# Head-mixing attention and a gated feed-forward on one core: another order for the first loads, another place for the decoding of w_out, another draw of the planner

## The chip, the cores and the metric

One core of a Trainium2 chip runs one program. The metric is the device time of one execution in microseconds (us). Lower is better.

## The reference

Twelve attention heads are mixed with each other by two small 12 x 12 matrices, once ahead of the softmax and once behind it. The result goes through a two-layer feed-forward whose weights are 64-bit floating-point numbers.

```
q, k, v: 4 batches x 12 heads x 448 tokens x 64        w_pre, w_post: 12 x 12
scores = scale * q @ k^T                   (per head)
scores = einsum('bhij,hg->bgij', scores, w_pre)
attn   = softmax(scores, axis=-1)
attn   = einsum('bhij,hg->bgij', attn, w_post)
x      = (attn @ v), heads put side by side            1792 tokens x 768
h      = x @ w_in                                       768 x 2048
g      = h * clip(h + 3, 0, 6) / 6
out    = g @ w_out                                      2048 x 768
```

## The kernel before

**Work and tiles.** The attention runs in 32 units of about 60 tokens (8 per batch). For a unit `m` and each of 3 pairs of head pairs `p`, `scores` multiplies queries by keys on TensorE (L448), copies the result to an SBUF tile `s` (L470 and L471 for the first two units, on ACT and DVE; L473 on ACT for the rest) and sends it by DMA (L480) into `T_two` or `T_one`, where the heads of one token stand in neighbouring partitions. Twelve such sends of 105 KB make up a unit. Even units use `T_two`, odd ones `T_one`. `step` then takes tokens in tens: the mix ahead of the softmax on TensorE (L533), the maximum of each row on DVE (L541, `nb`), the exponential on ACT (L542), the scaling on POOL (L551), from step 24 on a split into two fp16 numbers (L553 ACT, L554 POOL), the mix behind it on TensorE (L570), and the copy into `AR` (L579 DVE, L581 ACT). `av` multiplies by v (L607). `moe1` is the first feed-forward product (L828), its results go to device memory (`gd`). The second product is L1109: seven products of halves in place of eight, for which sums and differences of blocks of w_out are stored (`wsd`) and read back.

**Weights.** The 64-bit weights are decoded on the core. `w_in_item` loads one of 16 pieces of 786 KB (L354) into a buffer `stw` of which there are two; `decode` takes one ACT pass (L676) and four DVE passes (L679, L683, L687, L691). `w_out_decode` does the same for 24 pieces of 524 KB, with further DVE sums (L781) and stores (L778). Both weights and the first loads of `g` share the two `stw` buffers.

**What sets the order.** Nothing is written in the order in which it runs. Every operation is handed to `Plan` with an engine, a planned duration and a priority (a lower number goes first; most are the step's number plus an offset). `Plan.schedule` walks through planned time and gives each engine, whenever it is free, the ready operation with the lowest number. The result is a fixed order for each engine, the DMA queue of SP among them, in which every transfer waits behind the one ahead of it. Two settings bend the order: `DRAWS`, the seed of a random addition of up to 0.3 to every priority, and `STAY`, by how much TensorE may prefer an operation of the kind that it has just done.

**Fillers.** Where the planner sees TensorE idle between planned us 9 and 150, `filler` puts in matmuls of 512 columns on an identity matrix (L873) that compute nothing. Their number is fixed when the program is built.

**The start.** `mixes` loads the two small matrices and the identity; `keys(0)` and `queries(0, 0)` load the first batch's keys in four transfers and the first queries in two, of which the first holds unit 0 and the second unit 1. Ahead of all that TensorE runs ten matmuls on zeros (L856). `mixes_post` brings the maximum of w_post across partitions with one matmul (`across`, L379, `wst`).

Of the kernel before, what the change touches and what calls it, by code (L numbers as in the profile page):

```python
# [14 lines left out]
F32 = mybir.dt.float32  # L15
# [3 lines left out]
AF = mybir.ActivationFunctionType  # L19
# [8 lines left out]
P = 128  # L28
# [33 lines left out]
DRAWS, JITTER = (3,), 0.3  # L62
AV_BY = 1
Z_AT = 30
LAT_0, ACT_T = 1.0, 1
# [54 lines left out]
class Plan:  # L120
# [7 lines left out]
    STAY = (8.0,)  # L128
# [176 lines left out]
def body(ctx: ExitStack, tc: tile.TileContext, q4, kT, vj, wpre0, wpost0, ident0, w_in, w_out, outT):  # L305
# [85 lines left out]
    def mixes():  # L391
        dma(32768, lambda: SP.dma_start(wpre8(), wpre0), [], [wpre8], -11)
        dma(30720, lambda: SP.dma_start(wpost_n(), wpost0), [], [wpost_n], -10.9)
        dma(32768, lambda: SP.dma_start(ident(), ident0), [], [ident], -10.8)
        dve(0.2, lambda: DVE.tensor_scalar(wpre8(), wpre8(), 1.0 / 8.0, None, op0=ALU.mult), [], [wpre8], -6)
# [16 lines left out]
    def keys(b):  # L412
        for j in range(2):
            t = buf(one, [P, 3, S], F32, f"ks{j}", f"ks_{b}_{j}")
            ks[b, j] = t
            for lo, hi in ((0, 2), (2, 3)) if j == 0 else ((0, 1), (1, 3)):
                (bulk if b or j else dmas)(229376 * (hi - lo), lambda lo=lo, hi=hi, t=t: t()[:, lo:hi], kT[b, :, 3 * j + lo:3 * j + hi],
                                           [(t, i) for i in range(lo, hi)], b * STEPS - 30 + 3 * j + lo if b else -14 + 3 * j + lo)

    def queries(b, c, at, after=()):  # L420
        t = buf(rot, [P, QX], F32, "qx", f"qx_{b}_{c}", 2)
        qs[b, c] = t
        if b + c:
            bulk(P * QX * 4, t, q4[b, c], [t], at, after)
        else:
            for i, (lo, hi) in enumerate(((0, 6 * CU + 4), (6 * CU + 4, QX))):
                dmas(P * (hi - lo) * 4, lambda lo=lo, hi=hi: t()[:, lo:hi], q4[b, c, :, lo:hi], [(t, i)], at + 2.5 * i, after)
# [23 lines left out]

    def scores(m, p, at):
# [16 lines left out]
        if m < 2:  # L469
            act(0.48, lambda: ACT.activation(st()[:, 0], at2[0](), AF.Copy), [ps[0]], [(st, 0)], at + 0.5)  # L470
            dve(0.57, lambda: DVE.tensor_copy(st()[:, 1], at2[1]()), [ps[1]], [(st, 1)], at + 0.5)  # L471
        else:
            act(0.9, lambda: ACT.activation(st(), two()[:, :, :S], AF.Copy), ps, [(st, 0), (st, 1)], at + 0.5)  # L473
        parts = [(0, 10, 6, 0)] if n < 7 else [(0, 10, 2, 0), (20, 5, 2, 2)]
        for cc in range(2):
            for u in range(2):
                h = 2 * (2 * p + cc) + u
                for q0, r, t, t0 in parts:
                    def go(cc=cc, u=u, h=h, q0=q0, r=r, t=t, t0=t0):
                        (ACT if m < ACT_T and u else SP).dma_start(T()[4 + h:4 + h + 12 * (r - 1) + 1:12, t0:t0 + t], st()[D * cc + q0:D * cc + q0 + r * t, u, :])  # L480

                    plan.op("ACT" if m < ACT_T and u else "SP", 0.77, go, [(st, u), T_zero[m % 2]], [(T, (h, t0))], at + 0.7, (), t * 30700, lat=LAT_T if m else LAT_0)
# [394 lines left out]

    plan.filler = filler
    mixes()
    keys(0)  # L880
    queries(0, 0, -13.5)
    for m in range(2):
        for p in range(3):
            scores(m, p, -10 + 8 * m + 1.6 * p)
        if m == 0:
            mixes_post(last_qk)
    for fc in range(EARLY):
        w_in_item(fc)
    FU = [m // 8 * STEPS + 6 * (m % 8) for m in range(NU)]
# [3 lines left out]
    for s in range(NS + 12):  # L893
# [21 lines left out]
        if s in range(WO_AT, WO_AT + WO_BY * WO_EARLY, WO_BY):  # L915
            w_out_decode((s - WO_AT) // WO_BY, 2000 + 10 * (s - WO_AT) // WO_BY, [t_load[s]])
# [312 lines left out]
```

## Time and profile before

| | us |
|---|---|
| median of 3 runs | 797.62 |
| fastest and slowest of them | 796.53, 798.78 |
| the profiled execution | 795.99 |
| its span | 794.2 |
| TensorE busy in it | 774.1 |
| DVE, ACT, POOL busy | 581.2, 527.1, 369.9 |

The span runs from the first to the last instruction of the core; 1.8 us of the profiled execution lie around it. Busy times are those of instructions that compute; issuing a DMA and waiting are not counted. A line such as L533 is a line of the kernel before; in the kernel with the change the same code stands some lines further down (L350 is L351, L480 is L482, L533 is L541, L873 is L881).

### The profile page before, as it was taken

How to read it: one execution, taken by the hardware profiler on the slowest of the kernel's cores; microseconds unless marked ns; L12 is line 12 of the kernel's file. 1: busy time of each engine (PE TensorE's matmuls, PEld its weight loads, DVE VectorE, ACT ScalarE, POOL GpSimd, SP SyncE). 2: the span in 40 equal slices, each digit the busy share in tenths (PEclk: the TensorE clock that was granted, in tenths of full speed). 3: DMA queues.
4: the chain of work that ended last, by engine and by line, in shares of the span. 5: the costliest groups of instructions: out<-in, count | busy, mean ns of one | idle time of the engine just before them, and what ended most of it. 6: DMA issues, size and time to landing. Idle time of an engine off the chain costs nothing.

```text
span 794.2 us, 28021 instructions
## 1 busy us (share of the span) xinstructions
PE 774.1 (97%) x11616; PEld 627.0 (79%) x11616; DVE 581.2 (73%) x1152; ACT 527.1 (66%) x1044; POOL 369.9 (47%) x535
## 2 busy tenths in 40 slices
PE   6999999999999999999999999999999999999998
PEld 2566676678677777777787777768999999999998
DVE  2799796688969368778756678777777599898622
ACT  2588888698998658988775788896676474243200
POOL 2357789479988327767562676886100000000000
PEclk9999999999999999999999999999999999999999
DMA  7766654766365578665746676644599674654101
GB/s 232 211 214 197 204 172 119 215 221 210 90 191 154 155 248 272 209 184 171 231 149 232 193 228 198 197 128 142 178 350 369 215 238 126 186 158 145 42 17 50
DMA packets 100815, 147.75 MB, mean 186 GB/s; under 512 B 9840, under 2 KB 79824, under 8 KB 100688
## 3 DMA queue, kind: packets, MB, share of 16 engines
q1 hardware_dynamic: 100268, 145.31, 58.9%
q8 instruction: 91, 1.49, 0.8%
q10 hardware_dynamic: 420, 0.65, 0.3%
q14 instruction: 36, 0.29, 0.1%
HBM read 76.02 MB, written 31.20 MB: 135 GB/s over the span
## 4 chain that ended last, share of the span: by engine, by line
PE 76%; DMA 7%; DVE 6%; ACT 6%; POOL 2%; issue 2%; SPq 1%; ACTq 0%; POOLq 0%; DVEq 0%
PE single L1109 24%; PE single L828 20%; PE single L570 8%; PE single L607 7%; PE pair L448 7%; PE single L533 6%; PE single L873 3%; DMA T_two<-s 2%; DMA wsd_P<-WF 2%; ACT e L542 2%; DVE nb L541 2%; SPq L480 1%; ACT s L473 1%; ACT eh L553 1%; POOL e L551 1%
## 5 line engine op out<-in xcount | busy, mean ns | idle before, releaser
L828 PEld LDWEIGHTS <-wi 128*128 128x128 f16 x2304 | 213.1, 98 | 24.2 <-issue 18.4
L828 PE MATMUL single<-x,wi 128*128 128x208 f16 (+1 forms) x2304 | 228.5, 259 | 2.0 <-ACT e L542 0.9
L554 POOL TENSOR_TENSOR el<-e,eh 128x448 f16<-128x448 f32 x156 | 168.3, 1097 | 32.0 <-ACT eh L553 30.0
L551 POOL TENSOR_SCALAR e<-e,r 128x448 f32<-128x448 f32 x180 | 129.8, 731 | 39.4 <-DVE r L545 34.4
L1109 PEld LDWEIGHTS <-ws_P 128*128 128x128 f16 x1440 | 138.0, 98 | 0.0
L542 ACT ACTIVATE e<-single,nb 128x448 f32<-128x448 f32 x180 | 113.8, 641 | 20.2 <-DVE nb L541 19.9
L541 DVE TENSOR_REDUCE nb<-single 128x1 f32<-128x448 f32 x180 | 102.9, 614 | 18.5 <-PE single L533 11.0
L553 ACT ACTIVATE eh<-e 128x448 f16<-128x448 f32 x156 | 88.0, 584 | 16.6 <-POOL e L551 16.0
L841 ACT ACTIVATE g<-single,three,uh 128x240 f32<-128x240 f32 (+1 forms) x128 | 68.8, 542 | 41.5 <-PE single L828 41.0
L473 ACT ACTIVATE s<-pair 128x896 f32<-128x896 f32 x90 | 82.9, 921 | 16.4 <-PE pair L448 11.7
L448 PE MATMUL pair<-ks,qx 64*64 64x448 f32 x728 | 89.5, 554 | 3.7 <-ACT s L473 3.6
L843 DVE SCALAR_TENSOR_TENSOR g<-g,six,single 128x240 f32<-128x240 f32 (+1 forms) x128 | 56.2, 442 | 41.3 <-ACT g L841 40.9
L570 PEld LDWEIGHTS <-eh 60*128 60x128 f16 x2496 | 66.3, 100 | 22.3 <-issue 21.4
L607 PEld LDWEIGHTS single<-AR,v 128*64 128x64 f32 (+1 forms) x1536 | 66.8, 136 | 14.3 <-issue 5.2
L607 PE MATMUL single<-AR,v 128*64 128x120 f32 (+3 forms) x1536 | 72.3, 263 | 0.6 <-ACT e L542 0.3
L570 PE MATMUL single<-wpost_h,eh 60*128 60x60 f16 x1248 | 72.4, 202 | 0.3 <-DVE x L633 0.3
L570 PE MATMUL single<-wpost_h,el 60*128 60x60 f16 x1248 | 72.3, 202 | 0.0
L570 PE MATMUL single<-wpost_l,eh 60*128 60x60 f16 x1248 | 72.1, 202 | 0.0
L1109 PE MATMUL single<-gx_P,ws_P 128*128 128x224 f16 x720 | 69.3, 259 | 0.0
L579 DVE TENSOR_SCALAR AR<-single 128x480 f32<-128x480 f32 (+1 forms) x92 | 57.9, 639 | 11.9 <-PE single L570 11.8
L581 ACT ACTIVATE AR<-single 128x480 f32<-128x480 f32 (+1 forms) x92 | 53.5, 586 | 18.7 <-PE single L570 18.7
L544 POOL TENSOR_SCALAR sm<-sm 128x2 f32<-128x2 f32 (+1 forms) x92 | 26.6, 289 | 82.3 <-ACT e L542 77.1
(240 smaller groups left out, 1161.1 us busy)
## 6 DMA issues: line engine op xcount, KB each, us to landing
T_two<-s SPq DMA_DIRECT2D x186, 105.0 KB
T_one<-s SPq DMA_DIRECT2D x144, 105.0 KB
wi<-in_w_in SPq DMA_DIRECT2D x16, 768.0 KB
wo<-in_w_out SPq DMA_DIRECT2D x24, 512.0 KB
wsd_P<-WF SPq DMA_DIRECT2D x42, 256.0 KB
wP<-wsd_P SPq DMA_DIRECT2D x36, 256.0 KB
gd<-g SPq DMA_DIRECT2D x32, 240.0 KB
gd<-g SPq DMA_DIRECT2D x32, 208.0 KB
```

The source lines that it names most:

```text
L448: PE.matmul(at[u]()[cc * D:cc * D + D], q()[r, o:o + D], ks_[cc]()[r, pr % 3, :], start=True, stop=True)
L473: act(0.9, lambda: ACT.activation(st(), two()[:, :, :S], AF.Copy), ps, [(st, 0), (st, 1)], at + 0.5)
L541: dve(0.53, lambda r=r: DVE.tensor_reduce(nb()[:, r:r + 1], ps[r]()[:, :S], axis=AX.X, op=ALU.max, negate=True), [ps[r]], [(nb, r)], s + 0 ...
L542: act(0.62, lambda r=r: ACT.activation(e()[:, r], ps[r]()[:, :S], AF.Exp, bias=nb()[:, r:r + 1], accum_out=sm()[:, r:r + 1]), [ps[r], (nb, ...
L551: pool(0.63, lambda r=r: POOL.tensor_scalar(e()[:, r], e()[:, r], rr()[:, r:r + 1], 1.0, op0=ALU.mult, op1=ALU.mult), [rr], [(e, r)], s + ...
L553: act(0.47, lambda r=r: ACT.activation(eh()[:, r], e()[:, r], AF.Copy), [(e, r)], [(eh, r)], s + 0.65 + 0.3 * r)
L554: pool(1.02, lambda r=r: POOL.tensor_tensor(el()[:, r], e()[:, r], eh()[:, r], op=ALU.subtract), [(e, r), (eh, r)], [(el, r)], s + 0.7 + 0 ...
L570: PE.matmul(out, x()[rows, r, js], z()[rows], start=(i == 0), stop=(i == len(mix) - 1))
L607: PE.matmul(pss[run]()[u * D:(u + 1) * D, k:k + N], v()[rows, jc, g * D:(g + 1) * D], cols(jc * H + g, rows), start=start, stop=stop)
L828: PE.matmul(pv(), wi_g[g]()[:, w, f0, cc, :], x()[:, z, cc, :n], start=(cc == 0 and i == 0), stop=(cc == 5 and i == 2))
L841: act(0.44, lambda fc=fc, pv=pv, r=r: ACT.activation(r(), pv(), AF.Relu, bias=three()[:, fc:fc + 1], scale=uh()[:, fc:fc + 1]), [ps, (thre ...
L1109: PE.matmul(ps()[:, :NH], w_view(w, y, 2 * m + i)[:, f], g(x)[:, f, :], start=(i == 0 and f == 0 and (y, x) == (0, 0)), stop=(i == 1 and f ...
```

## The change

Priorities, after-conditions and settings change; no computation is added or taken away.

- The first half of the first queries (unit 0) stays in front; the second half (unit 1) waits for the last of the first keys and for the third send of unit 0 to have been issued. The small matrices go behind all four transfers of keys, and the planner now reckons with the same landing time for all four.
- The sends of unit 0 are handed to the planner after all three scores. Five of the twelve (`ACT_0`) are issued by ACT, and only after ACT's last copy of that unit; before, ACT issued the six with `u` = 1, each behind its own copy.
- The first piece of w_in waits for the tenth send of unit 0 to have been issued.
- The decoding of w_out has the priority of its step plus 8, where it had 2000 and more, which put it behind everything else of its engine.
- `DRAWS` goes from 3 to 9 and `STAY` from 8 to 6.

```diff
-DRAWS, JITTER = (3,), 0.3
+DRAWS, JITTER = (9,), 0.3
...
-LAT_0, ACT_T = 1.0, 1
+WO_LAG = 8
+LAT_0, ACT_0, WI_0, QB_0 = 1.0, (5, 7, 8, 10, 11), 9, 2
...
-    STAY = (8.0,)
+    STAY = (6.0,)
...
     def mixes():
-        dma(32768, lambda: SP.dma_start(wpre8(), wpre0), [], [wpre8], -11)
-        dma(30720, lambda: SP.dma_start(wpost_n(), wpost0), [], [wpost_n], -10.9)
-        dma(32768, lambda: SP.dma_start(ident(), ident0), [], [ident], -10.8)
+        dma(32768, lambda: SP.dma_start(wpre8(), wpre0), [], [wpre8], -9.5)
+        dma(30720, lambda: SP.dma_start(wpost_n(), wpost0), [], [wpost_n], -9.3)
+        dma(32768, lambda: SP.dma_start(ident(), ident0), [], [ident], -9.4)
...
-                (bulk if b or j else dmas)(229376 * (hi - lo), lambda lo=lo, hi=hi, t=t: t()[:, lo:hi], kT[b, :, 3 * j + lo:3 * j + hi],
+                (bulk if b else dmas)(229376 * (hi - lo), lambda lo=lo, hi=hi, t=t: t()[:, lo:hi], kT[b, :, 3 * j + lo:3 * j + hi],
...
     def queries(b, c, at, after=()):
-        t = buf(rot, [P, QX], F32, "qx", f"qx_{b}_{c}", 2)
-        qs[b, c] = t
+        t = qs[b, c] = qs.get((b, c)) or buf(rot, [P, QX], F32, "qx", f"qx_{b}_{c}", 2)
...
-            for i, (lo, hi) in enumerate(((0, 6 * CU + 4), (6 * CU + 4, QX))):
-                dmas(P * (hi - lo) * 4, lambda lo=lo, hi=hi: t()[:, lo:hi], q4[b, c, :, lo:hi], [(t, i)], at + 2.5 * i, after)
+            lo, hi = (6 * CU + 4, QX) if after else (0, 6 * CU + 4)
+            dmas(P * (hi - lo) * 4, lambda: t()[:, lo:hi], q4[b, c, :, lo:hi], [(t, int(lo > 0))], at, after)
...
-                    plan.op("ACT" if m < ACT_T and u else "SP", 0.77, go, [(st, u), T_zero[m % 2]], [(T, (h, t0))], at + 0.7, (), t * 30700, lat=LAT_T if m else LAT_0)
+                    def send(eng="SP", after=(), go=go, u=u, h=h, t=t, t0=t0):
+                        return plan.op(eng, 0.77, go, [(st, u), T_zero[m % 2]], [(T, (h, t0))], at + 0.7, after, t * 30700, lat=LAT_T if m else LAT_0)
+                    if m:
+                        send()
+                    else:
+                        sends.append(send)
...
+    def behind(o, x=None):
+        x = x or plan.ops[-1]
+        o.order.append(x)
+        x.n += 1
...
         if m == 0:
+            first_act.update(ACT_0)
+            sent = [send("ACT", first_copy) if h in first_act else send() for h, send in enumerate(sends)]
+            queries(0, 0, -9, [keys_op])
+            behind(sent[QB_0])
             mixes_post(last_qk)
     for fc in range(EARLY):
+        n_ops = len(plan.ops)
         w_in_item(fc)
+        behind(sent[WI_0], plan.ops[n_ops])
...
-            w_out_decode((s - WO_AT) // WO_BY, 2000 + 10 * (s - WO_AT) // WO_BY, [t_load[s]])
+            w_out_decode((s - WO_AT) // WO_BY, s + WO_LAG if WO_LAG else 2000 + 10 * (s - WO_AT) // WO_BY, [t_load[s]])
```

What the planner makes of it is read from the order of the two built programs. First SP's queue from its fifth transfer on (`in_kT`, `in_q`, `in_w_in` are keys, queries and w_in in device memory; `s_0` to `s_2` are the scores of the three p). Before:

```order
L392 DMA wpre_107<-in_wpre 128x64
L350 DMA qx_0_100<-in_q 128x360
L393 DMA wpost_n<-in_wpost 128x60
L394 DMA ident<-in_ident 128x128
L354 DMA ks_1_103<-in_kT 128x896
L354 DMA qx_1_122<-in_q 128x724
L354 DMA wi_124<-in_w_in 128x768
L480 DMA T_two<-s_0_126 10x6x448 x2
L480 DMA T_two<-s_1_141 10x6x448 x2
L480 DMA T_two<-s_2_160 10x6x448 x2
L354 DMA qx_2_182<-in_q 128x724
```

With the change:

```order
L351 DMA ks_1_103<-in_kT 128x896
L393 DMA wpre_108<-in_wpre 128x64
L395 DMA ident<-in_ident 128x128
L394 DMA wpost_n<-in_wpost 128x60
L355 DMA qx_1_116<-in_q 128x724
L482 DMA T_two<-s_0_123 10x6x448 x4
L351 DMA qx_0_98<-in_q 128x360
L482 DMA T_two<-s_1_133 10x6x448 x2
L482 DMA T_two<-s_2_149 10x6x448
L355 DMA wi_172<-in_w_in 128x768
L482 DMA T_one<-s_0_185 10x6x448 x4
```

The second half of the first queries (360 columns) was the sixth transfer and stands behind four sends now; the piece of w_in stood ahead of every send and stands behind SP's seven.

Second, TensorE at the start, around the matmul on `wst` (`single` and `pair` are PSUM banks; a line of `ident` alone, L873 or L881, is a filler; `qx_0` are the first queries). Before, from the last scores of unit 1 on:

```order
L448 MATMUL single_147<-ks_1_103,qx_0_100 64x448
L448 MATMUL single_149<-ks_1_103,qx_0_100 64x448
L448 MATMUL single_147<-ks_1_103,qx_0_100 64x448
L448 MATMUL single_149<-ks_1_103,qx_0_100 64x448
L448 MATMUL pair_117<-ks_0_98,qx_1_122 64x448 x4
L379 LDWEIGHTS wst
L379 MATMUL single_154<-ident,wst 128x128
L873 LDWEIGHTS ident
L873 MATMUL single_156<-ident 128x512
```

With the change, from the last scores of unit 0 on:

```order
L448 MATMUL single_136<-ks_1_103,qx_0_98 64x448
L448 MATMUL single_138<-ks_1_103,qx_0_98 64x448
L380 LDWEIGHTS wst
L380 MATMUL single_146<-ident,wst 128x128
L448 MATMUL single_175<-ks_0_100,qx_0_98 64x448
L448 MATMUL single_85<-ks_0_100,qx_0_98 64x448
L448 MATMUL single_175<-ks_0_100,qx_0_98 64x448
L448 MATMUL single_85<-ks_0_100,qx_0_98 64x448
L881 LDWEIGHTS ident
L881 MATMUL single_127<-ident 128x512
L448 MATMUL single_127<-ks_0_100,qx_0_98 64x448
```

The one matmul on `wst` stood behind the scores of unit 1 and stands ahead of them; up to the first L533 (L541 with the change) there were 24 fillers and are 9 now. Over the whole program there were 110 and are 109; no other count of a TensorE instruction differs.

Third, DVE in the second batch (`nb` is the maximum of a row, `WF` with `wo` the decoding of w_out). Before:

```order
L541 TENSOR_REDUCE nb_4480<-single_149 128x1
L541 TENSOR_REDUCE nb_4480<-single_147 128x1
L679 TENSOR_SCALAR WF,wo_st<-WF 128x512
L683 TENSOR_SCALAR WF<-WF 128x512
L687 SCALAR_TENSOR_TENSOR WF<-wo_4244,WF 128x512
L843 SCALAR_TENSOR_TENSOR g_14_4514<-g_14_4514,six,single_85 128x240
L691 SCALAR_TENSOR_TENSOR WF<-wo_4244,WF 128x512
L843 SCALAR_TENSOR_TENSOR g_14_4514<-g_14_4514,six,single_156 128x240
L579 TENSOR_SCALAR AR<-single_137 128x48x10
```

With the change:

```order
L687 TENSOR_SCALAR WF,wo_st<-WF 128x512
L691 TENSOR_SCALAR WF<-WF 128x512
L851 SCALAR_TENSOR_TENSOR g_14_4558<-g_14_4558,six,single_175 128x240
L695 SCALAR_TENSOR_TENSOR WF<-wo_4108,WF 128x512
L549 TENSOR_REDUCE nb_4616<-single_146 128x1
L549 TENSOR_REDUCE nb_4616<-single_136 128x1
L699 SCALAR_TENSOR_TENSOR WF<-wo_4108,WF 128x512
L851 SCALAR_TENSOR_TENSOR g_14_4644<-g_14_4644,six,single_85 128x208
L789 TENSOR_TENSOR WF<-WF 128x512
```

A pass of the decoding stood behind the maxima of its time and between the results of `moe1`; now passes stand ahead of maxima as well. Along the whole order a maximum follows directly on such a pass at 10 places before and at 27 with the change.

## Rows read from the trace of the kernel before

**Rows 1.** The page, part 1: busy time, share of the span, instructions.

```profile
span 794.2 us, 28021 instructions
...
PE 774.1 (97%) x11616; PEld 627.0 (79%) x11616; DVE 581.2 (73%) x1152; ACT 527.1 (66%) x1044; POOL 369.9 (47%) x535
```

**Rows 2.** Windows by stage: stretch, length, then busy PE, PEld, DVE, ACT, POOL; clock, DMA, GB/s.

```profile
0.00:23.00 23.00, 15.98 (x93) 5.63 (x93) 8.20 (x23) 5.12 (x8) 4.83 (x7) 1.00 0.72 224
23.00:52.00 29.00, 29.00 (x334) 17.46 (x333) 24.33 (x57) 19.48 (x41) 12.78 (x26) 1.00 0.75 224
52.00:151.00 99.00, 96.55 (x1493) 64.57 (x1491) 79.62 (x185) 82.45 (x164) 77.23 (x121) 1.00 0.58 178
151.00:572.00 421.00, 413.38 (x7401) 320.42 (x7400) 312.21 (x665) 331.88 (x714) 275.09 (x382) 1.00 0.62 191
572.00:794.20 222.20, 219.17 (x2307) 218.91 (x2305) 156.88 (x226) 88.19 (x120) 0.00 (x0) 1.00 0.54 171
```

**Rows 3.** TensorE by line: busy us, mean ns; idle before, and its releasers.

```profile
L873 PE MATMUL single<-ident 128*128 128x512 bf16 x110 | 26.6, 380 | 0.0
```

**Rows 4.** Timeline of the start: start, us, engine, line, tiles, count [idle before <-releaser].

```profile
1.17 4.45 PE L856 MATMUL single<-warm 128*128 128x512 f16 x10 [1.17 <-DVE warm L854]
...
6.54 0.92 PE L448 MATMUL single<-ks,qx 64*64 64x448 f32 x8
...
7.36 8.87 SPq L480 DMA_DIRECT2D T_two<-s  x6
...
9.28 2.57 PE L448 MATMUL single<-ks,qx 64*64 64x448 f32 x24 [1.82 <-DMA ks<-in_kT]
...
12.59 0.98 PE L448 MATMUL single<-ks,qx 64*64 64x448 f32 x8 [0.74 <-ACT s L470]
...
14.69 2.28 ACTq L480 DMA_DIRECT2D T_two<-s  x2
...
17.61 0.22 PE L379 MATMUL single<-ident,wst 128*128 128x128 bf16 x1 [3.29 <-ACT s L470]
...
17.67 3.83 PE L873 MATMUL single<-ident 128*128 128x512 bf16 x17
...
19.82 0.95 DVE L679 TENSOR_SCALAR_CACHE_REDUCE WF<-WF 128x768 f32<-128x768 f32 x1
...
23.00 2.49 PE L533 MATMUL single<-T_two,wpre 64*64 64x448 f32 x24
...
30.31 3.18 SPq L480 DMA_DIRECT2D T_two<-s  x4
```

**Rows 5.** Windows of the first transfers; the last column is GB/s moved.

```profile
2.00:9.00 7.00, 5.46 (x25) 1.66 (x23) 1.38 (x4) 0.55 (x1) 3.36 (x3) 1.00 0.95 315
```

**Rows 6.** The chain that ended last: start, us, what; issue of a DMA to its landing.

```profile
117.71 1.18 DMA T_one<-s
...
443.85 2.28 DMA T_two<-s
...
457.46 3.61 DMA qx<-in_q
```

**Rows 7.** A window with the decoding of w_in, columns as in rows 2.

```profile
40.00:80.00 40.00, 39.77 (x522) 25.74 (x515) 37.93 (x92) 33.01 (x65) 26.23 (x48) 1.00 0.67 208
```

**Rows 8.** Waits of TensorE: us in total, times, longest.

```profile
PE pair L448 <- ACT s L473: 3.6, 4, 1.4
```

**Rows 9.** Timeline of TensorE at two of these places, columns as in rows 4.

```profile
215.15 0.98 PE L448 MATMUL pair<-ks,qx 64*64 64x448 f32 x8 [1.35 <-ACT s L473]
...
444.55 0.98 PE L448 MATMUL pair<-ks,qx 64*64 64x448 f32 x8 [1.03 <-ACT s L473]
```

**Rows 10.** DVE pass L687 of the decoding, and who waited for it (us, times).

```profile
L687 DVE SCALAR_TENSOR_TENSOR WF<-wo,WF x24: 666/688/1410, 237.7 to 550.8; 128x512 int32<-128x512 int32 x24
...
who waited for it (us, times):
  PEld single L533: 0.2, 1
```

More of the change, by code (lines that the diff above doesn't have):

```diff
@@ L450, in products @@
         return mm
+    sends, first_copy, first_act = [], [], set()
     def scores(m, p, at):
@@ L469, in scores @@
         if m < 2:
-            act(0.48, lambda: ACT.activation(st()[:, 0], at2[0](), AF.Copy), [ps[0]], [(st, 0)], at + 0.5)
+            first_copy[:] = [act(0.48, lambda: ACT.activation(st()[:, 0], at2[0](), AF.Copy), [ps[0]], [(st, 0)], at + 0.5)]
             dve(0.57, lambda: DVE.tensor_copy(st()[:, 1], at2[1]()), [ps[1]], [(st, 1)], at + 0.5)
@@ L479, in go @@
                     def go(cc=cc, u=u, h=h, q0=q0, r=r, t=t, t0=t0):
-                        (ACT if m < ACT_T and u else SP).dma_start(T()[4 + h:4 + h + 12 * (r - 1) + 1:12, t0:t0 + t], st()[D * cc + q0:D * cc + q0 + r * t, u, :])
-                    plan.op("ACT" if m < ACT_T and u else "SP", 0.77, go, [(st, u), T_zero[m % 2]], [(T, (h, t0))], at + 0.7, (), t * 30700, lat=LAT_T if m else LAT_0)
+                        (ACT if m == 0 and h in first_act else SP).dma_start(T()[4 + h:4 + h + 12 * (r - 1) + 1:12, t0:t0 + t], st()[D * cc + q0:D * cc + q0 + r * t, u, :])
+                    def send(eng="SP", after=(), go=go, u=u, h=h, t=t, t0=t0):
[4 more added lines that the diff above has]
+                        sends.append(send)
     vs = {}
@@ L878, in body @@
     plan.filler = filler
+    def behind(o, x=None):
+        x = x or plan.ops[-1]
+        o.order.append(x)
+        x.n += 1
     mixes()
     keys(0)
+    keys_op = plan.ops[-1]
     queries(0, 0, -13.5)
```

## The prediction, made before the kernel with the change was run

> **What bounds the kernel now.** I read the page's busy times first. TensorE works 774.1 of 794.2 us [rows 1]; no other engine comes near. The windows by stage show where the other 20.1 us lie [rows 2]: 7.02 before the first L533 at 23.00, none from 23 to 52, 2.45 up to 151, 7.62 from 151 to 572, 3.03 behind. TensorE runs its instructions in a fixed order, so its time is the work it is given plus what it waits. Part of the work is filler, 110 matmuls for 26.6 us [rows 3], all before 151.
>
> The timeline of the start names the first 7.02 us [rows 4]: 1.17 until the zeros are there, 1.82 for the last keys, 0.74 for a copy by ACT, 3.29 ahead of the matmul on `wst`. That last wait is for a PSUM bank: ACT should empty it, but stands in an issue of sends that begins at 14.69 and takes 2.28. Then come 24 fillers, the first 17 in 3.83 us, and L533 starts at 23.00 without idle time ahead of it: it waits for fillers, not for its data.
>
> **The accounting.** The change computes nothing more or less; only one filler goes, 26.6/110 = 0.24 us. So the time moves by 0.24 us and by what TensorE waits more or less, wherever else work is moved to. An earlier first L533 is worth nothing by itself: 15 fillers are gone ahead of it and 14 have come back behind it.
>
> **First loads.** Some 0.28 MB (second half of the queries 0.184, small matrices 0.095) leave the queue ahead of the last keys. At the 315 GB/s of that stretch [rows 5] this is 0.9 us, so the wait of 1.82 becomes 0.9 (bounds 0 and 1.82). TensorE ends the scores of p = 1 at 6.54 + 0.92 = 7.46 [rows 4] and would end those of unit 0 at 7.46 + 0.9 + 0.95 = 9.3.
>
> **Sends and the second half of the queries.** ACT now finishes its three copies before it issues a send, and the bank for `wst` is free, as unit 1 has not taken it; the waits of 3.29 and 0.74 go. What is late next is unit 1, whose queries now stand behind four sends. SP begins to send at 7.36; four take 3.18 when nothing stops them [rows 4], so the queries are issued at 10.6. Their landing is not to be seen in the trace. The nearest rows are transfers of the chain: 1.18 from issue to use for one send on a quiet queue, 2.28 for another, 3.61 for queries of twice the size [rows 6]. I take 2.3, since this transfer is half as large and behind a few sends, and keep 11.8 and 14.2 as ends around 12.9. The wait is then 12.9 - 9.3, less 0.2 for the matmul on `wst`: 3.4 us (2.3 to 4.7). The start waits 1.17 + 0.9 + 3.4 = 5.5 in place of 7.0: **-1.6 us**, between -2.7 and -0.3.
>
> T_two is not late behind that. SP's seven sends and the queries end near 13.4, ACT's five near 14.0 (five by 0.8 from 10.0), and with 2.28 the last lands by 16.3. TensorE needs until 12.9 + four groups of scores at 0.9 + nine fillers at 0.225 (3.83/17) = 18.5. The first L533 comes near 18.5.
>
> **The clock.** The stretch without work from 9.3 to 12.9 calls for a look at it. The record of the granted clock says 1.00 in every stage [rows 2], though for the first microseconds it can't be taken at its word: behind the idle 3.29 us the fillers ran at 225 ns for 512 columns, while the first ten matmuls of the same width took 445 ns (4.45/10) [rows 4]. These are its two levels, 2.4 and 1.2 GHz. An idle stretch of that size was survived, so I charge nothing. The Trainium skill, in "TensorE: Matmul & The Clock Gate", Part 1, says against this change that half rate is the default and that TensorE falls back to it after sitting idle; by that rule the new stretch would be answered with half rate. The row of the idle 3.29 us does not bear it out here, but its fillers show the clock only after it ended; the case is kept as a rival below.
>
> **The first piece of w_in.** Its 0.786 MB now follow SP's seven sends. Its decoding on DVE ran ahead of the first maxima (its first pass of 0.95 begins at 19.82 [rows 4]), in time that DVE had to spare; now it comes behind them. That brings some 3 us of DVE work into the stage in which DVE is busy 37.93 of 40 us [rows 7]. The fillers that came back stand there. I cost it at nothing because TensorE is covered by them; without that cover it eats the gain of the start (rival 2).
>
> **Seed and STAY.** Scores have one pair of banks, which ACT must copy out before the next scores; TensorE waited 3.6 us in 4 places for that [rows 8]. Two of the four (1.35 and 1.03 us [rows 9]) stand where less than 2 us of other matmuls lie between two groups of scores. There are 22 such places before and 16 now. 2.4 x 6/22 = **-0.65 us**; bounds -3.6 (all gone) and +1.2 (one more of their mean length). The other waits behind 52 us are short and of many kinds; another draw moves them, and I see no direction: 0, give or take 3.
>
> **Decoding of w_out.** With its higher priority a maximum stands directly behind a pass of it at 27 places, before at 10. A pass takes 0.69 (median 688 ns [rows 10]). Nobody on TensorE waited for that pass for more than 0.2 us in all, although it often stood ahead of other work. From that 17 more places are worth 17 x 0.2/10 = 0.34: **+0.3 us**; the ends are 0 and 17 x 0.69 = 11.7. I stand near the low one because from 230 us on TensorE has L828 in hand, which does not wait for maxima. A gain is possible as well, since a w_out piece frees its buffer sooner and SP's queue stands behind such buffers; it is inside the 3 us above.
>
> **Sum.** -0.24 - 1.6 - 0.65 + 0.3 = -2.2 us. The profiled execution took 795.99, of which 1.8 lie around the span; the median of the runs shown is 1.63 higher, at 797.62. The difference is carried over to the median: 797.6 - 2.2 = **795.4**. A measurement of this kernel can tell about 0.3%, 2.4 us, from no change, so the forecast lies just inside.
>
> **Rivals.**
> 1. *All of it is kept.* The queries land at 11.8 (-2.7) and the waits for the bank pair mostly go (-3): 797.6 - 0.2 - 2.7 - 3 = 791.7. For it: DVE and ACT are 73% and 66% busy [rows 1], so the rest could follow. Against it: DVE is full from 40 to 80.
> 2. *DVE paces the second stage.* The first L533 is 4.5 us earlier, but DVE has 3 us more to do behind it, and the fillers fill the rest; TensorE waits behind 23 us what it saved before. 797.6 - 0.2 = 797.4. For it: 37.93 of 40 [rows 7]. The case in which the new priority of w_out changes nothing ends here too: its loads stand at nearly the same places in SP's queue.
> 3. *Slower: the decoding stands ahead of the maxima.* At the 17 places the maximum, the exponential and the mix behind it are late by one pass. If TensorE has less than 0.69 us of other matmuls there in half of them, 17 x 0.69/2 = 5.9 us: 795.4 - 0.3 + 5.9 = 801.0. It decides from some 8 uncovered places on. For it: DVE runs its order as it stands and is busy 312 of 421 us from 151 on [rows 2]. Against it: the 0.2 us above [rows 10].
> 4. *Slower: the clock.* Four groups of scores and nine fillers, 3.6 + 2.0 us, would double: 795.4 + 5.6 = 801.0.
>
> **How the numbers follow.** The forecast has 0.42; its own range is 793 to 798, 0.19 of it below 795.2 and 0.23 above. Rival 1 has 0.21, rival 2 0.16, rival 3 0.16, rival 4 0.05. Faster: 0.19 + 0.21 = 0.40; within 0.3%: 0.23 + 0.16 = 0.39; slower: 0.21. The range of 790 to 801 takes in rivals 1 to 3 up to their values and leaves out less than 2 in 10.
>
> **What would show it.** In the timeline of the changed kernel: the wait for keys at 0.9, none ahead of `wst` but one of some 3.4 us ahead of the scores of unit 1, the first L533 near 18.5 without idle time. In the windows: 5.5 us of waiting before it, none up to 52 (rival 2: 1 to 2 us of it by 80). Among TensorE's waits: less than 3.6 us for the bank pair, and DVE's maxima or the exponentials not above 2 us (rival 3: more than 5, between 230 and 550). Fillers at 225 ns from the first on (rival 4: 445). I am wrong if TensorE's busy time moves by more than 1 us, because then work does not cost the same in another order, or if its waiting outside the start moves by more than 4.

## The result, and the profile after

| | before | with the change |
|---|---|---|
| median, us (6 runs each) | 798.2 | 803.37 |
| fastest and slowest, us | 795.27, 799.79 | 802.31, 808.48 |
| ratio to before, 95% interval | | 1.0078 [1.0053, 1.0104] |
| the profiled execution, us | 795.99 | 802.57 |
| its span, us | 794.2 | 800.8 |
| TensorE busy in it, us | 774.1 | 776.9 |

The kernel is 0.78% slower, some 6.2 us, and its median lies above the forecast range (790 to 801). The forecast was 2.2 us faster. The profiled execution shows 6.6 us more of span, so it can be read as it stands. The page's first part answers to [rows 1]:

```profile
span 800.8 us, 28033 instructions
...
PE 776.9 (97%) x11615; PEld 626.8 (78%) x11615; DVE 586.6 (73%) x1152; ACT 528.1 (66%) x1044; POOL 370.4 (46%) x535
```

TensorE is 2.8 us longer at work and waits 3.8 us more (794.2 - 774.1 = 20.1 before, 800.8 - 776.9 = 23.9 now). The windows by stage answer to [rows 2], with the first window ending at the first mix (L541, L533 before):

```profile
0.00:21.87 21.87, 14.19 (x77) 4.43 (x77) 5.52 (x16) 4.54 (x7) 4.83 (x7) 0.84 0.66 214
21.87:52.00 30.13, 29.97 (x323) 17.72 (x322) 23.41 (x49) 18.62 (x39) 10.10 (x21) 1.00 0.65 211
52.00:151.00 99.00, 96.18 (x1431) 63.74 (x1428) 81.30 (x187) 80.27 (x160) 74.68 (x120) 1.00 0.57 177
151.00:572.00 421.00, 411.43 (x7422) 316.57 (x7424) 313.56 (x668) 330.19 (x709) 280.83 (x388) 1.00 0.61 188
572.00:800.80 228.80, 225.11 (x2382) 224.34 (x2372) 162.81 (x234) 94.44 (x129) 0.00 (x0) 1.00 0.55 175
```

The waits are the length less the first number: 7.68, 0.16, 2.82, 9.57 and 3.69 us, against 7.02, 0, 2.45, 7.62 and 3.03. The first window also has a granted clock of 0.84 where [rows 2] had 1.00. What happened there stands in the timeline of the start, with the columns of [rows 4]:

```profile
5.58 0.98 PE L448 MATMUL pair<-ks,qx 64*64 64x448 f32 x8 [0.43 <-DMA ks<-in_kT]
...
6.36 1.30 PE L448 MATMUL single<-ks,qx 64*64 64x448 f32 x8
...
7.19 3.43 SPq L482 DMA_DIRECT2D T_two<-s  x4
...
7.86 0.98 PE L448 MATMUL single<-ks,qx 64*64 64x448 f32 x8 [0.21 <-DMA ks<-in_kT]
...
8.77 0.23 PE L380 MATMUL single<-ident,wst 128*128 128x128 bf16 x1
...
8.96 5.01 ACTq L482 DMA_DIRECT2D T_two<-s  x5
...
10.67 0.49 SPq L351 DMA_DIRECT2D qx<-in_q  x1
...
14.87 1.77 PE L448 MATMUL single<-ks,qx 64*64 64x448 f32 x8 [5.87 <-DMA qx<-in_q]
...
16.57 0.61 PE L881 MATMUL single<-ident 128*128 128x512 bf16 x1
...
17.11 2.24 PE L448 MATMUL single<-ks,qx 64*64 64x448 f32 x16
...
20.04 1.90 PE L881 MATMUL single<-ident 128*128 128x512 bf16 x8
...
21.87 2.49 PE L541 MATMUL single<-T_two,wpre 64*64 64x448 f32 x24
```

The waits for keys are 0.43 and 0.21 us in place of 1.82, and the matmul on `wst` waits for nothing (3.29 before). Then TensorE stands still for 5.87 us, because the second half of the queries, issued at 10.67, is not there before 14.83. The chain that ended last gives it as one piece (start, us, what; the time is that from the issue to the landing):

```profile
10.67 4.16 DMA qx<-in_q
```

Behind the standstill 8 matmuls of the scores take 1.77 us where they took 0.98 at 7.86, and one filler takes 0.61. The windows of this stretch say why (the last three columns are the granted clock, the DMA share and GB/s):

```profile
8.00:11.00 3.00, 1.00 (x9) 0.16 (x6) 2.46 (x11) 0.77 (x2) 0.00 (x0) 1.00 0.38 105
11.00:15.00 4.00, 0.13 (x4) 0.13 (x8) 0.11 (x1) 0.00 (x0) 0.00 (x0) 0.55 0.60 193
15.00:18.00 3.00, 3.00 (x17) 0.67 (x21) 0.62 (x1) 0.54 (x1) 0.00 (x0) 0.50 0.56 160
```

The granted clock is 0.55 while TensorE waits and 0.50 behind it: half of 2.4 GHz. At 20.04 eight fillers take 1.90 us, the rate of full clock, so it is back. The same windows show what the late load met: from 11 to 15 us the transfers move 193 GB/s with the engines 60% busy, where the first loads had 315 GB/s at 0.95 [rows 5]. What moves here are sends to ten partitions each, and the queries stand among them: in 4.16 us at that rate 0.80 MB move, the load's 0.18 and some six sends. That the sends around it delayed the load is worked out from these rows; no run here takes the sends away.

The waits of TensorE, with the columns of [rows 8]:

```profile
PE single L448 <- DMA qx<-in_q: 5.9, 1, 5.9
PE pair L448 <- ACT s L475: 3.9, 8, 1.2
PE single L836 <- ACT e L550: 1.9, 4, 0.9
...
PE single L836 <- POOL wi L754: 1.1, 1, 1.1
```

And TensorE by line, columns as in [rows 3]: 109 fillers take 27.3 us where 110 took 26.6.

```profile
L881 PE MATMUL single<-ident 128*128 128x512 bf16 x109 | 27.3, 382 | 1.2 <-ACT e L550 1.2
...
L448 PE MATMUL single<-ks,qx 64*64 64x448 f32 x40 | 6.3, 692 | 6.1 <-DMA qx<-in_q 5.9 <-DMA ks<-in_kT 0.2
```

The scores of the first two units (`single`) took 4.5 us before and take 6.3 now. Of these 1.8 us, 1.3 are the half clock (1.77 and 2.24 at 14.87 and 17.11, against 0.98 and 1.73 for the same matmuls in experiment 3); 0.4 fall on the eight at 6.36, which took 1.30 and not 0.92 because keys still came in while they ran.

One cut orders all that follows, at the start of the first mix. Before: 23.00 us up to it and 771.20 behind it, of which TensorE works 758.1 and waits 13.1. Now: 21.87 and 778.93, with 762.7 and 16.2. So the first mix came 1.13 us earlier, not 4.5, and 7.73 us came on behind it: 14 more fillers at 0.225 (3.2), 3.1 of waits and 1.4 of other work.

### The profile page after: what moved, and what is told of

It reads as the page before. It is cut to its first block, busy times and chain, and to the rows that moved or that the text cites. A ratio compares the mean times of both kernels' runs of the same rounds, so it can differ in the third digit from the quotient of the medians.

```text
span 800.8 us, 28033 instructions
## 1 busy us (share of the span) xinstructions
PE 776.9 (97%) x11615; PEld 626.8 (78%) x11615; DVE 586.6 (73%) x1152; ACT 528.1 (66%) x1044; POOL 370.4 (46%) x535
## 4 chain that ended last, share of the span: by engine, by line
PE 67%; DMA 11%; DVE 9%; SPq 5%; ACT 4%; issue 3%; POOL 1%; ACTq 0%; DVEq 0%; POOLq 0%
PE single L1130 23%; PE single L836 16%; PE single L578 8%; PE single L615 6%; PE pair L448 5%; PE single L541 4%; SPq L482 4%; DMA wi<-in_w_in 3%; PE single L881 3%; DMA wo<-in_w_out 2%; DVE nb L549 2%; DMA qx<-in_q 1%; DVE WF L695 1%; DVE AR L587 1%; DMA ks<-in_kT 1%
## 5 line engine op out<-in xcount | busy, mean ns | idle before, releaser
L562 POOL TENSOR_TENSOR el<-e,eh 128x448 f16<-128x448 f32 x156 | 174.6, 1138 | 39.8 <-ACT eh L561 37.4
L559 POOL TENSOR_SCALAR e<-e,r 128x448 f32<-128x448 f32 x180 | 127.5, 719 | 26.5 <-DVE r L553 24.6
L475 ACT ACTIVATE s<-pair 128x896 f32<-128x896 f32 x90 | 82.7, 919 | 14.9 <-PE pair L448 10.6
L615 PEld LDWEIGHTS single<-AR,v 128*64 128x64 f32 (+1 forms) x1536 | 66.5, 136 | 11.3 <-ACT eh L561 3.7
L552 POOL TENSOR_SCALAR sm<-sm 128x2 f32<-128x2 f32 (+1 forms) x92 | 24.6, 268 | 105.6 <-ACT e L550 99.9
```

Source lines behind the costliest of these rows:

```text
L559: pool(0.63, lambda r=r: POOL.tensor_scalar(e()[:, r], e()[:, r], rr()[:, r:r + 1], 1.0, op0=ALU.mult, op1=ALU.mult), [rr], [(e, r)], s + ...
L562: pool(1.02, lambda r=r: POOL.tensor_tensor(el()[:, r], e()[:, r], eh()[:, r], op=ALU.subtract), [(e, r), (eh, r)], [(el, r)], s + 0.7 + 0 ...
L615: PE.matmul(pss[run]()[u * D:(u + 1) * D, k:k + N], v()[rows, jc, g * D:(g + 1) * D], cols(jc * H + g, rows), start=start, stop=stop)
```

## The experiments

All ratios are to runs of the kernel before on the same chip, with 95% intervals. The last three columns are of the one profiled execution: where the first mix began, and what TensorE worked and waited from there to the end (windows up to and from the first mix). Each kernel has only one such execution, so single microseconds of these columns can be its own. The diffs leave out blank lines and the hook that applies an edit to the finished order.

| kernel | ratio | first mix, us | work behind it | waits behind it |
|---|---|---|---|---|
| before | 1 | 23.00 | 758.1 | 13.1 |
| the change | 1.0078 [1.0053, 1.0104] | 21.87 | 762.7 | 16.2 |
| 1 queries in front again | 0.9993 [0.9973, 1.0013] | 17.94 | 762.3 | 14.0 |
| 2 queries late in the kernel before | 1.0062 [1.0030, 1.0094] | 27.24 | 758.5 | 11.7 |
| 3 the wait filled with matmuls | 1.0026 [0.9996, 1.0057] | 20.05 | 761.0 | 16.6 |
| 4 old priority of w_out | 1.0080 [1.0049, 1.0111] | 21.89 | 761.3 | 17.4 |
| 5 new priority of w_out alone | 0.9986 [0.9960, 1.0012] | 26.29 | 757.6 | 12.4 |
| 6 new draw alone | 1.0187 [1.0138, 1.0235] | 23.42 | 766.9 | 21.6 |
| 7 new start alone | 1.0010 [0.9983, 1.0037] | 22.79 | 763.4 | 11.6 |
| 8 as 7, queries in front | 1.0004 [0.9974, 1.0034] | 17.74 | 766.0 | 14.6 |
| 9 as 8, new priority of w_out | 0.9982 [0.9958, 1.0005] | 17.65 | 765.8 | 12.3 |
| 10 as 9, more fillers | 1.0040 [1.0013, 1.0067] | 18.35 | 766.2 | 13.4 |
| 11 as 1, fewer fillers | 1.0024 [0.9994, 1.0055] | 18.77 | 758.5 | 21.7 |
| 12 before, fewer fillers | 1.0023 [0.9988, 1.0058] | 21.58 | 758.1 | 17.8 |

**1. Queries in front again.** The finished order of the changed kernel, with one transfer moved: the second half of the first queries goes ahead of the next load of queries, which is ahead of all sends. Nothing else moves.

```diff
             behind(sent[QB_0])
+            second = plan.ops[-1]
+            def forward(out):
+                x = next(z for z in out if z[1] is second)
+                out.remove(x)
+                i = next(i for i, z in enumerate(out) if isinstance(z[1], Op) and z[1].bytes == P * QX * 4)
+                out.insert(i, x)
+            plan.edits.append(forward)
```

> The kernel with the change, one instruction moved: the second half of the first queries goes back ahead of the third load of queries and of all sends; every engine's order is otherwise the same. Theory A (the late queries): the wait of 5.87 us ahead of the scores of unit 1 and the half clock behind it cost 5.4 and 2 us and nothing hides them; without them TensorE starts its first mix near 15.5 instead of 21.9 and the time falls from 803.4 to 796 or 797. Theory B (DVE and ACT pace what follows): TensorE is early at the first mix but waits again before 150 us; the time stays at 801 or more. Theory C (the new order behind 150 us, decoding ahead of maxima included): what is left above the kernel before is 2 to 4 us, in the waits from 151 to 572.

Measured: 798.76 us, ratio 0.9993 [0.9973, 1.0013]. The timeline of the start:

```profile
8.87 0.23 PE L383 MATMUL single<-ident,wst 128*128 128x128 bf16 x1
9.03 0.98 PE L451 MATMUL single<-ks,qx 64*64 64x448 f32 x8
...
12.68 1.90 PE L884 MATMUL single<-ident 128*128 128x512 bf16 x8
17.94 2.49 PE L544 MATMUL single<-T_two,wpre 64*64 64x448 f32 x24 [3.35 <-DMA T_one<-s]
```

The wait for the queries is gone and the scores of unit 1 follow at 9.03. A new wait of 3.35 us stands ahead of the first mix, for sends: its row names one into `T_one`, while the mix reads `T_two`, whose last send is issued at 14.51 (kernel 8 names `T_two` at the same place). So the first mix is not at the expected 15.5, and the time not at 796 or 797. It begins 3.93 us earlier than with the change, and behind it 2.7 us less are needed, most of it waits (16.2 to 14.0). Under this draw, the place of this one transfer carries the whole slowdown of the changed kernel. It does not show a gain: without it the change is worth nothing that can be told from no change.

**2. Queries late in the kernel before.** The opposite: the order of the kernel before, with that transfer moved behind SP's third send and the piece of w_in.

```diff
     queries(0, 0, -13.5)
+    second = plan.ops[-1]
+    def back(out):
+        x = next(z for z in out if z[1] is second)
+        out.remove(x)
+        at = [i for i, z in enumerate(out) if isinstance(z[1], Op) and z[1].bytes == 6 * 30700]
+        out.insert(at[5] + 1, x)
+    plan.edits.append(back)
```

> The kernel before with one instruction moved the other way: the second half of the first queries goes behind the sixth send of unit 0, SP's third, and behind the piece of w_in; every order is otherwise the same. Theory A (the late queries by themselves): the scores of unit 1 wait 4 us or more, the clock falls to half behind that, and the time rises by 4 to 6 us, to 802 to 804. If later stages absorb it: 798 to 800.

Measured: 803.53 us, ratio 1.0062 [1.0030, 1.0094]. The timeline, and the same piece of the chain:

```profile
9.04 0.98 PE L451 MATMUL single<-ks,qx 64*64 64x448 f32 x8 [2.14 <-DMA ks<-in_kT]
16.46 4.71 PE L451 MATMUL single<-ks,qx 64*64 64x448 f32 x24 [6.43 <-DMA qx<-in_q]
...
27.24 0.98 PE L536 MATMUL single<-T_two,wpre 64*64 64x448 f32 x8
```

```profile
4.96 7.37 DMA wi<-in_w_in
...
12.36 4.06 DMA qx<-in_q
```

Again some 4 us from issue to landing, a wait of 6.43, and behind it 24 matmuls of scores in 4.71 us where [rows 4] has 2.57. The reason of the lateness is another in part: SP's queue stands from 10.62 until the piece of w_in lands at 12.33, and only then issues the queries; from there to the landing the transfers move 220 GB/s at 0.71. Both experiments show that late queries cost time; neither separates the sends from the other traffic.

**3. The wait filled.** The changed kernel with 22 matmuls on the identity ahead of unit 1's first scores. They compute nothing; the queries stay late.

```diff
+        if (m, p) == (1, 0):
+            score, bank = last_qk[0], ps[0]
+            def busy():
+                for _ in range(22):
+                    PE.matmul(bank()[:, :].rearrange("p (a b) -> p a b", a=4), ident(), ident().unsqueeze(1).broadcast_to([P, 4, P]), start=True, stop=True)
+            plan.edits.append(lambda out: out.insert(next(i for i, z in enumerate(out) if z[1] is score), (0.0, busy)))
```

> The kernel with the change, with 22 matmuls of 512 columns that compute nothing put ahead of the scores of unit 1, where TensorE waits 5.87 us for queries. They fit into the wait (22 x 0.22 = 4.8 us), so the wait itself stays. If the half clock costs 2 us by itself: the granted clock stays at full, the four groups of scores behind the wait take 0.95 in place of 1.8 and 1.1 us, and the time falls by about 2 us, to 801.4. If the clock is only a symptom and later waits absorb it: 803 as it was.

Measured: 800.72 us, ratio 1.0026 [0.9996, 1.0057].

```profile
8.88 4.91 PE L479 MATMUL single<-ident 128*128 128x512 bf16 x22
14.57 0.98 PE L451 MATMUL single<-ks,qx 64*64 64x448 f32 x8 [0.77 <-DMA qx<-in_q]
...
15.80 1.73 PE L451 MATMUL single<-ks,qx 64*64 64x448 f32 x16
...
20.05 2.49 PE L553 MATMUL single<-T_two,wpre 64*64 64x448 f32 x24
```

The queries still come late (14.57), but the scores run at full clock (0.98, and 16 in 1.73), and the first mix begins 1.82 us earlier than with the change. Between the centres, 0.52 of the 0.78% goes, about two thirds; the two intervals just overlap, so the share is rough. It is more than the 1.4 us of half clock at the start would give, and the queries came 0.3 us sooner in this execution.

**4. Old priority of w_out** in the changed kernel (`WO_LAG = 8` becomes `0`), and **5. new priority alone** in the kernel before:

```diff
-            w_out_decode((s - WO_AT) // WO_BY, 2000 + 10 * (s - WO_AT) // WO_BY, [t_load[s]])
+            w_out_decode((s - WO_AT) // WO_BY, s + 8, [t_load[s]])
```

> The kernel with the change, with the decoding of w_out put back to its old priority (2000 and more); the first half of TensorE's order is the same as with the change. Theory A: no gain, 803 within 1 us. Theory C (decoding ahead of maxima costs): the waits between 230 and 570 us shrink by 2 to 3 us, and so does the time, to 800 or 801.

> The kernel before, with only the decoding of w_out at its step plus 8. Fillers stay at 110, the first three quarters of TensorE's order stay as they were. If decoding ahead of maxima costs: 800 or more, in waits behind 230 us. If it is neutral or frees SP's queue sooner: 797 to 799.

Measured: 1.0080 [1.0049, 1.0111] and 0.9986 [0.9960, 1.0012]. Taking it out helps nothing and putting it in harms nothing. The profile of the fifth kernel brought something else, in the part that is the kernel before unchanged:

```profile
18.02 0.27 PE L379 MATMUL single<-ident,wst 128*128 128x128 bf16 x1 [3.27 <-ACT s L470]
18.09 6.71 PE L873 MATMUL single<-ident 128*128 128x512 bf16 x17
```

```profile
18.00:22.00 4.00, 3.98 (x11) 1.46 (x11) 3.30 (x11) 1.63 (x3) 0.00 (x0) 0.50 0.70 219
```

The wait ahead of `wst` is the 3.29 of [rows 4] (3.27 here), but the 17 fillers behind it take 6.71 us, not 3.83, at a granted clock of 0.50. TensorE's order is the same up to there, so the same wait was answered with full clock in one execution and with half clock in the other.

**6. New draw alone**: `DRAWS` 9 and `STAY` 6 in the kernel before.

> The kernel before, with only the seed (9) and STAY (6) of the change. It has 140 fillers in place of 110. By the accounting of the prediction 30 more fillers cost 7.3 us if no waiting goes in their place: 805. If the fillers only fill what would be waited for anyway, 798 to 800.

Measured (four executions): 813.61 us, ratio 1.0187 [1.0138, 1.0235], far slower, and more than the 7.3 us priced for 30 fillers. The planner put in 140 fillers, and the waits behind the first mix are 21.6 us, 11.3 of them between 151 and 300:

```profile
151.00:300.00 149.00, 137.70 (x2433) 98.92 (x2431) 101.90 (x229) 117.42 (x248) 106.43 (x157) 0.98 0.53 161
```

A draw is thus no small term, and it can't be priced apart from the start: under the new start with the queries in front it cost nothing that can be measured (kernel 1 against kernel 9, which differ in the draw alone, 0.9993 and 0.9982). Seed and `STAY` were never run apart from each other.

**7. New start alone**: the changed kernel with `DRAWS` 3, `STAY` 8 and `WO_LAG` 0, so the queries are late as before. **8.** The same with the queries in front, by the edit of kernel 1. **9.** Kernel 8 with `WO_LAG` 8.

> The kernel with the change, but with the old seed (3), the old STAY (8) and the old priority of w_out's decoding: only the start is changed. The planner now puts in 128 fillers where the change has 109. The late queries are in it as well. By the accounting (work plus waiting): 19 fillers at 0.24 are 4.6 us on top of what the late queries cost, 803 + 4 = 807, give or take 3 for the waits of another order. If fillers only stand where TensorE would wait anyway: 803.

> The kernel of e5 (start alone, old seed, old STAY, old priority of w_out) with the second half of the first queries in front again. If the late queries cost the same 4 to 5 us whatever the draw: 799.7 - 4.6 = 795, below the kernel before. If the later stages pace this order: 798 to 800 as e5.

> The kernel of e9 with the new priority of w_out's decoding, so the whole change but for the draw (seed 3, STAY 8) and with the queries in front. If the new draw of the change is worth nothing: 795 as e9. If the priority costs behind 230 us: 797 or more; e6 made that unlikely.

Measured: 1.0010 [0.9983, 1.0037], 1.0004 [0.9974, 1.0034] and 0.9982 [0.9958, 1.0005]. Kernel 7 waits 5.83 us for the queries and still loses nothing that can be measured, where 803 or 807 us were expected and 799.68 came:

```profile
15.01 1.77 PE L448 MATMUL single<-ks,qx 64*64 64x448 f32 x8 [5.83 <-DMA qx<-in_q]
```

Kernel 8 begins the first mix 5.05 us earlier and gains nothing either: behind it 5.75 us come on, 3.1 of waits and 2.7 of work. (Its profiled execution took 800.15 us, 1.3 above its median, so some of this is that execution's own.) Of that work 1.6 us are the first mix itself at half clock:

```profile
17.74 4.12 PE L544 MATMUL single<-T_two,wpre 64*64 64x448 f32 x24 [3.18 <-DMA T_two<-s]
```

```profile
14.00:17.74 3.74, 0.56 (x3) 0.10 (x2) 0.00 (x0) 1.12 (x3) 0.00 (x0) 0.99 0.57 166
17.74:21.80 4.06, 4.06 (x25) 1.40 (x25) 1.86 (x4) 1.39 (x5) 0.10 (x1) 0.59 0.77 275
```

A wait of 3.18 us ended in half clock here, one of 3.35 in kernel 1 did not (its first mix took 2.49). Kernel 9 has the lowest ratio of all, and its interval still holds 1; the 795 us expected of kernels 8 and 9 did not come.

**10. More fillers.** Kernel 9 with 16 more matmuls that compute nothing, ahead of the first mix, in the wait for `T_two`.

```diff
+            def bridge(out):
+                i = next(i for i, z in enumerate(out) if z[1] is last_pre[0])
+                j = max(k for k in range(i) if not isinstance(out[k][1], Op))
+                out[i:i] = [out[j], out[j]]
+            plan.edits.append(bridge)
```

> The preceding kernel of this series (the old draw, the queries in front, w_out's decoding at its step's priority; 797.3, ratio 0.9982) with 16 more matmuls that compute nothing ahead of the first mix, where TensorE waited 3.36 us for a send into T_two and where the first mix then ran at half clock (3.69 us in place of 2.49, from 18.8 to 22.2). Theory that the clock is what the start still loses: 16 at 0.225 = 3.6 us of matmuls take the place of the wait, the half clock goes, the first mix starts near 17.9 and takes 2.5, so some 1.0 us less in the span: ratio near 0.997 to before, and the interval wholly below 1. Rival, that later stages (DVE, the transfers) set the pace whatever the start does: the wait and the half clock go as well, but the waits behind 24 us grow by the same 1 us, ratio again 0.998. Second rival, the clock falls all the same at another place: half-clock stretch elsewhere, ratio 0.998 to 1.001.

Measured: 800.03 us, ratio 1.0040 [1.0013, 1.0067], slower.

```profile
12.96 5.35 PE L884 MATMUL single<-ident 128*128 128x512 bf16 x24
18.35 2.49 PE L544 MATMUL single<-T_two,wpre 64*64 64x448 f32 x24
```

```profile
300.00:450.00 150.00, 146.55 (x2463) 113.77 (x2463) 105.77 (x223) 112.08 (x240) 88.68 (x117) 0.98 0.66 209
```

The near half came as expected: no wait, and a first mix of 2.49 us. But it begins at 18.35, not at 17.9 and later than kernel 9 (17.65), and the clock is below full elsewhere (0.98 from 300 to 450). The second rival, a fall of the clock at another place (kernel 9 has 1.00 there), is nearest in the profile. But the medians differ by 2.7 us from kernel 9, more than it priced, and over all executions the granted clock averages 0.998 against 0.999, so the clock alone hardly parts them; why stays open.

**11. and 12. Fewer fillers**: kernel 1 and the kernel before, each with two matmuls less per group (69 and 75 fillers).

```diff
-            for _ in range(n + more):
+            for _ in range(max(0, n + more - 2)):
```

> The kernel of e1 (change with the queries in front) with two fillers less in every group, 69 in place of 109, every order otherwise the same. If TensorE is bound by the work it is given: 40 x 0.24 = 9.8 us less, of which the 8 fillers ahead of the first mix give nothing (it waits for its sends there), so 798.8 - 9 = 790. If DVE and ACT pace the stage up to 100 us (rival 2 of the prediction): waits come where the fillers were, 797 to 799. If idle stretches cost the clock: slower than 799, with the granted clock at half somewhere before 150 us.

> The kernel before with two fillers less in every group, 75 in place of 110. If TensorE is bound by the work it is given: 35 x 0.24 = 8.5 us less, 790. If DVE and ACT pace the stage: 797 to 799.

Measured: 1.0024 [0.9994, 1.0055] and 1.0023 [0.9988, 1.0058]. Neither came near the 790 us of a TensorE bound by its work. The waits show what takes the place of the work left out, first in kernel 1, then in kernel 11:

```profile
PE single L544 <- DMA T_one<-s: 3.4, 1, 3.4
PE pair L451 <- ACT s L478: 3.0, 8, 1.1
```

```profile
PE pair L451 <- ACT s L478: 6.9, 10, 1.5
PE single L544 <- DMA T_two<-s: 5.1, 1, 5.1
```

Kernel 11's first mix also runs at half clock behind its wait of 5.1 us (4.18 us). In kernel 12 the work behind the first mix is 758.1 us, as before, although 31 of the fillers there are gone, 7.0 us at 0.225. The granted clock is what fills it up: half clock for 13 us takes the place of some 6.5 (first the slices of the span in tenths of full clock, then one window):

```profile
PEclk9969999999999999999999999999999999999999
```

```profile
44.00:57.00 13.00, 13.00 (x95) 8.96 (x95) 6.57 (x23) 5.10 (x9) 2.92 (x8) 0.50 0.57 172
```

## Why the prediction was wrong

**The step that failed** is "Sends and the second half of the queries". Its issue was right (10.6 forecast, 10.67 measured), its landing was not: 2.3 us forecast, with 1.2 and 3.6 as ends, and 4.16 measured. It was no accident of one execution: kernels 3, 4 and 7, with the queries at the same place, have 3.68, 3.87 and 3.99. The rows that I had leaned on did not stand for it. The send of 1.18 had others issued right ahead of it (115.63 and 116.43), so it measured no quiet queue, and the chain that gave 3.61 holds a send of 8.41 us (from 448.22) that I left out of the ends. At the start the load stood among nine sends from two queues, at 193 GB/s. Unit 0's scores also ended 0.5 us sooner, so the wait was 5.87 and not 3.4 us. The other parts of the start saved 5.2 (1.18 for keys, 3.29 and 0.74 for ACT). Experiments 1 and 2 show from both sides that late queries cost 0.6 to 0.9%; under the new draw that is the whole slowdown. It is no fixed price: kernels 7 and 8 show no such cost under the old draw with the new start.

The same step had the last send into `T_two` land by 16.3. SP's seven sends ended at 16.27 and not at 13.4, and in kernels 1, 8 and 9, where the queries came in time, the first mix waited for sends until 17.65 to 17.94. The late scores hid that error.

**The clock** was charged nothing, and rival 4 came true at a smaller size. From 14.87 to the first mix 7.0 us passed where 5.6 were forecast: 1.4 for the half clock, not 5.6, since full clock was back before the last 8 fillers. The argument that an idle stretch of 3.29 us "was survived" rested on one execution; experiment 5 shows another execution of the same order in which it was not. The clock also parts the executions from each other: the six with the change had a granted clock of 0.989 to 0.996 over the whole span, and the lowest took longest (808.48 us at 0.989, 802.31 at 0.996). Their mean was 0.9935, that of kernel 3 0.9994, that of 105 executions of the kernel before 0.9978. Among these 105, a clock lower by 0.001 goes with some 0.83 us more (a straight line through them); at that rate the 0.0043 between the means are an estimated 3.6 of the 6.2 us. That is a correlation and no experiment, and part of the lower clock falls into the wait itself, where it costs nothing.

Together these two make 3.4 us: the first mix at 21.87 in place of 18.5.

**The rest behind the first mix** was forecast at 792.0 - 18.5 = 773.5 us and was 778.9: 5.4 more. Waits hold part of it: 16.2, against 13.1 before and 14.0 with the queries in front. So some of it goes with the late start, and experiment 1 measures both together. How a late start comes to longer waits behind it was not traced.

**Seed and STAY** were forecast at -0.65 with nothing else expected, give or take 3. Waits for the bank pair went from 3.6 to 3.9 us, in 8 places in place of 4: shorter each, not fewer. The stretch from 151 to 300 waits 149 - 143.35 = 5.65 us now, 2.9 before. Kernel 1 has 6.0 there, kernels 7, 8 and 9 with the old draw 2.9, 2.1 and 3.5, so these waits go with the draw and not with the late queries. Experiment 6, at +1.9%, lies far outside the bounds. The draw had been taken for a term that can be added; it is another order of the whole program, and its price depends on what it is combined with.

**The accounting** held as an identity (2.8 of work and 3.8 of waits are the 6.6), and its sentence that an earlier first mix is worth nothing by itself fits kernels 7 and 8, which differ by 5.05 us there and by 0.0006 in the ratio, though not the change and kernel 1 (3.93 us and 0.0085). As a price list it failed. Fillers left out give their time to waits and to a lower clock (11, 12), and fillers put into a wait gained in one place (3) and lost in another (10).

**What held.** Keys: 0.64 us of waits measured, 0.9 forecast. The waits of 3.29 and 0.74 for ACT: gone. The piece of w_in: 0.16 us of waits up to 52. The decoding of w_out: +0.3 forecast, no effect that experiments 4 and 5 could measure, so rival 3 (+5.9) fell, although the waits for the exponentials (`e`) sum to 3.8 us and not to at most 2. Of the two signs given for a wrong forecast the first came: TensorE's busy time moved by 2.8 us, more than 1.

**Open.** Why the late queries cost 0.85% under the new draw (the change against kernel 1) and nothing measurable under the old one with the new start (7 against 8, whose intervals still leave room for some 0.5%). The half clock of the first mix in kernel 8's profile is 1.6 us of it; the other 4.1 us that came back there have no single place.

## What to carry to other kernels

A small load that was moved behind narrow sends took 3.7 to 4.2 us to land in four kernels here, so take such a landing from a stretch with the same traffic, not from another part of the program; and a load that the next matmuls need belongs ahead of everything that does not need to be early. In a program with a fixed order whose main engine is 97% busy, judge a start by the end of the program: 5 us gained before the first mix came back behind it, as waits and as work, part of it at half clock. One profile that shows no fall of the clock behind an idle stretch does not show that the stretch is safe.

## What the runs showed of the hardware

**With narrow sends under way the DMA engines were part idle.** Between 11 and 15 us sends to 10 partitions and a load of 0.18 MB were all that was under way; the engines' share was 0.60 and the rate 193 GB/s, against 0.95 and 315 [rows 5] for a stretch of mostly loads over 128 partitions. No run here varied the width alone. The Trainium skill, in "DMA: Bandwidth & Descriptors", section "Why a DMA increments its semaphore by 16 and not by 1", says that a transfer uses the largest number of engines up to 16 that divides the outer sizes of both sides; for these sends, which read 60 rows and write 10 partitions, that is 10 of 16, an estimate of 0.62 for the share. By that rule, the trace agrees in this window (0.60).

**The same wait, another clock.** Idle stretches of TensorE and the granted clock right behind them: 6.43 us, 0.50 (kernel 2); 5.87 us, 0.50 (the change); 3.36 us, 0.66 over the first mix (kernel 9); 3.35 us, full (kernel 1); 3.18 us, 0.59 over the first mix (kernel 8); 3.27 us, 0.50 (kernel 5); 3.29 us, fillers at full rate (before, the same order as kernel 5 up to there). The Trainium skill, in "TensorE: Matmul & The Clock Gate", Part 1, says that the engine falls back to half rate after it has sat idle; and that what a kernel sees of it at its start varies from run to run. By that rule the 5.87 us are answered with half clock, and the rows agree; for the stretches of 3.2 to 3.4 us they show both answers, one of them in each of two executions of the same order.
